# A Fourier-mixing and gated-FFN kernel: the first chunk's work reordered, the chunk-end sums spread wider, and the PSUM seeds put ahead of a sigmoid

## The chip, the cores and the metric

The kernel runs on one core of one Trainium2 chip, in float32 throughout. The metric is the device time of one execution in microseconds (us). The kernel before took 1995.84 us, the median of three runs (1994.73 to 1996.15). Its profiled execution spans 1993.0 us from the first to the last instruction.

## The reference

The input `x` has 8 batches of 3008 rows and 256 features. It goes through a two-dimensional Fourier transform, of which the real part is kept, and then through a gated feed-forward block with 1536 hidden features:

```python
X = np.fft.fft(np.fft.fft(x, axis=1), axis=2).real      # 8 x 3008 x 256
gate = 1.0 / (1.0 + np.exp(-(X @ w_gate)))
val = X @ w_val
out = (gate * val) @ w_out
```

The weights may come as float64, which the kernel converts itself.

## The kernel before, in words

**Fourier part.** The transform over features is linear, so it is multiplied into `w_gate` and `w_val` once (function `merge`), which gives the matrices G1 and G2. Of the transform over the rows only half of the output rows are needed as two parts: `pk` (even) and `qk` (odd). A row k of the output uses P + Q and the mirrored row S-k uses P - Q, with P = pk G1 and Q = qk G2. Each batch therefore gives two tensors with 1505 columns, `pk` and `qk`.

**Chunks, groups, steps.** The 1505 columns are cut into 6 chunks of up to 252. One step of the main loop treats one block of 128 hidden features of one chunk, so a chunk has 12 steps, a batch 72 and the kernel 576. Three steps form a group, whose hidden values h go into one part of the output product.

**One step i** is spread over the engines and over neighbouring steps (the loop at L747). TensorE (PE) computes P for both gates (`front_a`, 8 matmul records pf<-pk), multiplies an older group into the output (`back` of step i-5, 10 records po<-h or po<-sf) and adds Q onto the same PSUM bank (`front_b`, 8 records pf<-qk). Between them P has to be copied away, because S-k needs P - Q: `part` writes it as `ae`. In batch 0, chunk 0 (i < 12) `ae` is made by VectorE (L518); afterwards by ScalarE (L515), and there the bank is also pre-loaded ("seeded") by ScalarE with an edge term (`seed`, L501). Then `gate_a` takes the sigmoid of row k on ScalarE (L534) and forms P - Q for the row S-k as `z` on VectorE (L536 in chunk 0, L539 later). `gate_b` multiplies (L551), takes the S-k sigmoid on ScalarE (L552) and multiplies again (L553). GpSimd (POOL) adds blocks of h into `sf` (L558).

**Output product.** Instead of a plain product a fast scheme with 15 products of 128 x 128 blocks per group is used. It needs sums of weight blocks (`forms`, 11 sums on GpSimd at L311 and 4 scaled copies on ScalarE at L313 for each of four groups), sums of h blocks (`H_SUMS`, L558) and, at the end of a chunk, 20 sums of output blocks (`C_SUMS`, L604), four 32 x 32 transposes (`flip`, L612) and stores (L621, L625). The output banks are copied out of PSUM into the tile `c` by ScalarE as they finish (L582).

**Chunk 0 is special.** In its 12 steps the weights still arrive. There are 18 weight pieces, called jobs here by their index j: two thirds of them go through `merge` (PE, matmuls ps<-...), one third are pieces of `w_out` for `forms`. Each is converted from float64 bits: two activations on ScalarE (`weight_parts`, L260 and L261), three operations on VectorE (`weight_join`, L270, L271, L273) and one add on GpSimd (L275). In the loop job j is converted in step j-9, merged in a later step, and the load of job j+3 is issued when the add of job j has freed its place.

**What sets the order.** All engine queues are in program order, written out by hand: the order of calls in the loop at L747 is the order of the queues. Between engines only semaphores order the work. The lists `use`, `pre`, `side` and `later` are dictionaries or lists of closures which the loop empties at given places in a step; `later` holds the chunk-end sums, of which three are issued per step. Buffers: 3 PSUM banks for pf and ps, 5 for po, one `c` tile (`cp`), one `os` tile (`op`).

Of the kernel before, what the change touches and what calls it, by code (L numbers as in the profile page):

```python
# [7 lines left out]
F32 = mybir.dt.float32  # L8
I32 = mybir.dt.int32
U32 = mybir.dt.uint32  # L10
AF = mybir.ActivationFunctionType
ALU = mybir.AluOpType
# [49 lines left out]
PRODUCTS = ((0, 12), (1, 11), (4, 9), (6, 4), (2, 13), (5, 5), (13, 0), (8, 6), (11, 2), (12, 8), (9, 3),  # L62
            (10, 10), (14, 1), (15, 7), (16, 14))
PLACE = (0, 1, 2, 5, 3, 4, 6, 7, 8, 9, 10, 11, 14, 13, 12)
C_SUMS = (((8, 1, 8, 0), (1, 1, 0, 0), (3, 3, 1, 0), (0, 0, 10, 1), (4, 4, 0, 1), (1, 6, 2, 0),
           (4, 4, 1, 0), (10, 14, 8, 1), (7, 7, 10, 0), (11, 0, 11, 0), (11, 11, 5, 0), (5, 5, 7, 1)),
          ((9, 9, 8, 0), (9, 13, 9, 1), (9, 9, 2, 0), (12, 9, 12, 0), (12, 11, 12, 1), (14, 9, 14, 0),
           (6, 11, 6, 0), (13, 13, 6, 1)))
OUT = (3, 12)

C_LAST = (((8, 1, 8, 0), 0), ((1, 1, 0, 0), 0), ((3, 3, 1, 0), 0), ((1, 6, 2, 0), 1), ((0, 0, 10, 1), 0),
          ((11, 0, 11, 0), 1), ((4, 4, 0, 1), 0), ((4, 4, 1, 0), 0), ((11, 11, 5, 0), 1),
          ((9, 9, 8, 0), 1), ((10, 14, 8, 1), 0), ((7, 7, 10, 0), 0), ((6, 11, 6, 0), 1),
          ((5, 5, 7, 1), 0), ((9, 13, 9, 1), 0), ((9, 9, 2, 0), 0), ((14, 9, 14, 0), 0),
          ((13, 13, 6, 1), 0), ((12, 9, 12, 0), 0), ((12, 11, 12, 1), 0))
HUGE = float((2 ** 24 - 1 - 2 ** 20) * 2.0 ** -7)


@with_exitstack
def kernel(  # L80
# [41 lines left out]
    zp = ctx.enter_context(tc.tile_pool(name="zp", bufs=2))  # L122
    hp = ctx.enter_context(tc.tile_pool(name="hp", bufs=3))
    sp = ctx.enter_context(tc.tile_pool(name="sp", bufs=2))
    cp = ctx.enter_context(tc.tile_pool(name="cp", bufs=1))
    op = ctx.enter_context(tc.tile_pool(name="op", bufs=1))
    psx = ctx.enter_context(tc.tile_pool(name="psx", bufs=8 - NB, space=PSUM))
    pso = ctx.enter_context(tc.tile_pool(name="pso", bufs=1, space=PSUM))
# [52 lines left out]
    ge = const.tile([P, 2, NFT], F32, name="ge")  # L181

    x8 = const.tile([NP, B - 1, 4, NQ], F32, name="x8")
    zero = const.tile([2, 1, NO], F32, name="zero")
    table = const.tile([2, 1], F32, name="table")
    tr = dram.tile([P, 2, NQ, NE + NO], F32, name="tr")
    ed = dram.tile([B, NK + 1], F32, name="ed")
# [23 lines left out]
    def weight_load(j):  # L211


        w, c = jobs[j]
        src = (moe_w_gate, moe_w_val, moe_w_out)[w]
        src = src[2 * c * P : 2 * (c + 1) * P, :] if w == 2 else src[:, c * WC : (c + 1) * WC]
        src = src.rearrange("(c p) f -> p c f", p=P)

        def some(n, pool, tag):

            if tag not in shared:
                shared[tag] = pool.tile([P, n * WC], F32, name=f"w{tag}", tag=tag)
            return shared[tag]

        def home(j):

            if j in (0, 1, 2, 3, 5):
                pool, tag = (hp, "h") if j < 3 else (sp, "sf")
                t = pool.tile([P, 6 * WC], F32, name="raw", tag=tag)
                return t[:, 0 : 4 * WC], t[:, 4 * WC :]  # L230
            if j in (4, 6, 9):
                t = wf[:, {4: 1, 6: 2, 9: 3}[j]].rearrange("p m n -> p (m n)")
                return t[:, 0 : 4 * WC], t[:, 4 * WC : 6 * WC]
            t = some(10, cp, "c")
            if j == 7:
                raw = pqp.tile([P, 4 * WC], F32, name="raw", tag="pk")
                return raw, t[:, 6 * WC : 8 * WC]
            return t[:, 0 : 4 * WC], t[:, 4 * WC : 6 * WC]

        if j < KEEP:  # L240
            raw, ws = home(j)
        else:
            both = some(24, xp, "x4").rearrange("p (i n) -> p i n", n=2 * WC)
            r, i = (j - KEEP) % 3 * 2, 6 + (j - KEEP) % 6
            raw, ws = both[:, r : r + 2].rearrange("p a n -> p (a n)"), both[:, i]
        raw = raw.bitcast(I32).rearrange("p (c f w) -> p c f w", c=2, w=2)
        ws = ws.rearrange("p (c f) -> p c f", c=2)
        WS[j] = ws
        if src.dtype == F32:
            nc.sync.dma_start(out=ws, in_=src)  # L250
        else:
            RAW[j] = raw
            nc.sync.dma_start(out=raw.rearrange("p c f w -> p c (f w)"), in_=src.bitcast(I32))
# [20 lines left out]
                                       op0=ALU.bitwise_and, op1=ALU.bitwise_or)  # L274
        nc.gpsimd.tensor_tensor(wi, wi, lo, op=ALU.add)  # L275

    WO = {}

    def weight_use(j, other=None):
        w, c = jobs[j]  # L280
        if w == 2:
            WO[c] = WS.pop(j)
            for g in range(NG):
                if (3 * g + 2) // 2 == c:
                    forms(g)
        else:
            merge(WS.pop(j), w, c, other)

# [13 lines left out]
    def forms(g):  # L302

        w = [WO[f // 2].rearrange("p f (a h j) -> p f h a j", h=2, j=TB)[:, f % 2]
             for f in range(3 * g, 3 * g + 3)]
        f = wf[:, g].rearrange("p m (a j) -> p m a j", j=TB)

        def block(i):
            return w[i // 2][:, i % 2] if i < 6 else f[:, i - 6]
        for i, (a, b, op) in enumerate(W_SUMS):  # L310
            nc.gpsimd.tensor_tensor(f[:, i], block(a), block(b), op=(ALU.subtract, ALU.add)[op])  # L311
        for i, (a, sign) in enumerate(W_COPIES):
            nc.scalar.mul(f[:, len(W_SUMS) + i], block(a), float(sign))  # L313


    W = {}
# [229 lines left out]
    def gate_b(i):  # L546

        n = cut(i)[2]
        p, fh = i // 3, i % 3
        z, h = Z.pop(i), H[p]  # L550
        nc.vector.tensor_tensor(h[:, fh, 0:n], h[:, fh, 0:n], PF.pop(i)[:, 1], op=ALU.mult)  # L551
        nc.scalar.activation(z[:, 0], z[:, 0], AF.Sigmoid)  # L552
        nc.vector.tensor_tensor(h[:, fh, n:], z[:, 0], z[:, 1], op=ALU.mult)  # L553
        if fh == 1:
            SF[p] = sp.tile([P, 6 * WC], F32, name="sf", tag="sf")[:, 0 : 8 * 2 * CH // 3].rearrange(
                "p (s n) -> p s n", s=8)
        for dst, a, b, op in H_SUMS.get(fh, ()):
            nc.gpsimd.tensor_tensor(block(p, dst), block(p, a), block(p, b),  # L558
                                    op=(ALU.subtract, ALU.add)[op])
# [5 lines left out]
    def back(p, part):  # L565
# [7 lines left out]
        for at_, (hb, wb) in list(enumerate(PRODUCTS))[part * 5 : part * 5 + 5]:  # L573
            t, j = divmod(PLACE[at_], 3)
            mm(PO[t][:, j * R : (j + 1) * R], wf[:, g, wb], block(p, hb), g == 0 and at_ % 3 == 0,
               g == NG - 1)
            if g == NG - 1 and at_ % 3 == 2:
                if t == 0:
                    C[0] = cp.tile([P, 10 * WC], F32, name="c", tag="c")
                    nc.gpsimd.memset(C[0][:, 15 * R : 15 * R + 40], 0.0)  # L580
                if not (last and t == NB - 1):
                    nc.scalar.copy(C[0][:, 3 * t * R : 3 * (t + 1) * R], PO[t][:, 0 : 3 * R])  # L582
        if part == 2:
            del H[p], SF[p]
            if g == NG - 1:
# [2 lines left out]
    def finish(b, c, last):  # L588
# [37 lines left out]
                                      in_=os_[0][a * TB : a * TB + m - full * TB, s, full].rearrange(  # L626
                                          "p h j -> p (h j)"))

        if last:
            for x, e in C_LAST:  # L630
                sum_(*x, engine=(nc.vector, nc.gpsimd)[e])
                if x[0] == 5:
                    flip(0, 0)
                    flip(1, 0)
            for half in range(2):
                flip(half, 1)
                store(half)
            return
        for h in range(2):
            later.extend([lambda x=x: sum_(*x) for x in C_SUMS[h]])  # L640
            later.append(lambda h=h: flip(0, h))
            later.append(lambda h=h: (flip(1, h), h and (store(0), store(1))))

    nc.gpsimd.memset(zero, 0.0)
    nc.scalar.activation(table, zero[:, 0, 0:1], AF.Sigmoid)
    nc.scalar.dma_start(out=dt, in_=dtab.rearrange("(c p) d -> p c d", p=P))  # L650
    for j in range(2):
        weight_load(j)
# [42 lines left out]
    def at(i, *fs):  # L695
        side.setdefault(i, []).extend(fs)
# [2 lines left out]

    pre, use = {}, {}  # L700
    for j in range(9, len(jobs)):
        pre.setdefault(j - 9, []).append(lambda j=j: weight_parts(j))
        at(j - 9, lambda j=j: weight_join(j))
        if KEEP <= j < len(jobs) - 3:
            at(j - 9, lambda j=j: weight_load(j + 3))
    for j in range(3, len(jobs)):
        w, c = jobs[j]
        use.setdefault(2 * c + (-3, -2, 1)[w], []).append(lambda j=j: weight_use(j))


    i0 = NFT
# [34 lines left out]

    for i in range(count):  # L747
        front_a(i)
        if i:
            gate_a(i - 1)  # L750
        part(i)
        if i:
            gate_b(i - 1)
        for f in use.pop(i, []):
            f()
        if i >= 5:
            back((i - 5) // 3, (i - 5) % 3)
        front_b(i)
        for f in pre.pop(i, []):
            f()  # L760
        for j in range(max(i0, i + 1), min(count, i + 3)):
            if j not in PF:
                seed(j)
        for f in later[0:3]:
            f()
        del later[0:3]
        for f in side.pop(i, []):
            f()
    gate_a(count - 1)
    gate_b(count - 1)  # L770
    for i in range(count, count + 5):
        back((i - 5) // 3, (i - 5) % 3)
    for f in later:
        f()


# [47 lines left out]
```

## Time and profile before

| | before |
|---|---|
| time, median of 3 | 1995.84 us |
| span of the profiled execution | 1993.0 us |
| TensorE busy | 1945.6 us (98%) |
| VectorE busy | 1538.4 us (77%) |
| ScalarE busy | 1395.6 us (70%) |
| GpSimd busy | 1627.1 us (82%) |
| mean granted TensorE clock | 0.993 |

A busy share is the share of the span in which an engine had an instruction in flight. The slices of the profile cut the span into 40 equal parts and give the same share for each. A table by windows gives busy time for stretches chosen by the reader, with the granted clock of TensorE. A timeline lists instructions in order of time; in square brackets stands how long the engine was idle before, and what ended that. Matmul records of one kind that follow each other are merged into one row with their number.

### The profile page before, as it was taken

The page shows a single profiled execution, that of the slowest core. Times are in us where ns is not written, and L with a number is a line of the kernel's source. Part 1 is how long each engine was busy: PE and PEld are TensorE (multiplying, and loading weights), DVE is VectorE, ACT ScalarE, POOL GpSimd, SP SyncE. Part 2 cuts the span into 40 slices and gives each one's busy share as a digit, 9 for nine tenths or more (in the row PEclk, how much of TensorE's full clock was granted, in tenths as well). Part 3 has the DMA queues.
Part 4 walks back from the last instruction along what each step waited for, and adds up shares of the span by engine and source line. Part 5 has one row for each costly group of instructions (what it writes and reads, how often), then busy time and mean ns, then how long its engine had stood idle before and what let it go on. Part 6 is the DMA issues. An engine that isn't in the chain of part 4 may idle for free.

```text
span 1993.0 us, 34353 instructions
## 1 busy us (share of the span) xinstructions
PE 1945.6 (98%) x11232; PEld 1793.0 (90%) x11232; DVE 1538.4 (77%) x3061; ACT 1395.6 (70%) x3198; POOL 1627.1 (82%) x2878
## 2 busy tenths in 40 slices
PE   6799999999999999999999999999999999999997
PEld 4689889998999899998999989999899999999997
DVE  7668778886788778787878877788678876877776
ACT  3467767776777667776777767777677776777775
POOL 3788988897888878897889878888788886777776
PEclk8999999999999999999999999999999999999999
DMA  7253413112012020211112021111210110011011
GB/s 266 86 132 90 139 29 109 45 25 80 14 46 56 16 77 14 60 44 49 43 25 79 15 77 24 45 49 20 79 19 14 20 21 14 14 23 18 14 21 24
DMA packets 171414, 101.40 MB, mean 51 GB/s; under 512 B 133860, under 2 KB 163172, under 8 KB 168556
## 3 DMA queue, kind: packets, MB, share of 16 engines
q1 hardware_dynamic: 169294, 98.64, 19.7%
q8 instruction: 88, 1.44, 0.3%
q10 hardware_dynamic: 1940, 0.56, 0.1%
q14 instruction: 92, 0.75, 0.1%
HBM read 74.39 MB, written 50.18 MB: 63 GB/s over the span
## 4 chain that ended last, share of the span: by engine, by line
PE 79%; DVE 12%; ACT 5%; POOL 2%; issue 1%; DMA 1%; SPq 0%; POOLq 0%; DVEq 0%; ACTq 0%
PE pf L131 40%; PE po L131 33%; DVE c L604 6%; PE ev L131 4%; DVE z L539 3%; DVE h L553 2%; ACT z L552 2%; ACT pf L501 1%; PE od L131 1%; ACT ae L515 1%; DMA x<-in_xf_dram 1%; POOL wf L311 1%; ACT c L582 1%; POOL sf L558 1%; PE ps L131 1%
## 5 line engine op out<-in xcount | busy, mean ns | idle before, releaser
L558 POOL TENSOR_TENSOR sf<-h 128x168 f32<-128x168 f32 (+1 forms) x960 | 540.4, 581 | 239.3 <-DVE h L553 239.3
L558 POOL TENSOR_TENSOR sf<-h,sf 128x168 f32<-128x168 f32 (+1 forms) x1152 | 644.9, 579 | 56.1 <-DVE h L553 56.1
L131 PE MATMUL pf<-qk,G 128*128 128x252 f32 (+1 forms) x2304 | 587.8, 378 | 7.7 <-DVE ae L518 4.3
L131 PE MATMUL pf<-pk,G 128*128 128x252 f32 (+1 forms) x2304 | 582.7, 376 | 0.0
L501 ACT ACTIVATE pf<-ek,ge 128x252 f32<-128x252 f32 (+1 forms) x1128 | 535.8, 475 | 18.4
L539 DVE TENSOR_TENSOR z<-ae,pf 128x504 f32<-128x504 f32 (+1 forms) x564 | 376.5, 668 | 221.2 <-ACT h L534 220.5
L604 DVE TENSOR_TENSOR c<-c 128x168 f32<-128x168 f32 (+1 forms) x950 | 520.9, 564 | 16.9 <-ACT c L582 3.6
L131 PE MATMUL po<-sf,wf 128*128 128x168 f32 (+1 forms) x3072 | 530.9, 306 | 0.0
L131 PEld LDWEIGHTS pf<-pk,G 128*128 128x128 f32 x2304 | 437.1, 190 | 51.8 <-issue 2.3
L131 PE MATMUL po<-h,wf 128*128 128x168 f32 (+1 forms) x2688 | 477.2, 306 | 6.2 <-POOL wf L311 4.6
L131 PEld LDWEIGHTS po<-sf,wf 128*128 128x128 f32 x3072 | 473.9, 190 | 8.4
L131 PEld LDWEIGHTS po<-h,wf 128*128 128x128 f32 x2688 | 428.2, 190 | 23.6 <-POOL wf L311 5.1
L131 PEld LDWEIGHTS pf<-qk,G 128*128 128x128 f32 x2304 | 408.3, 190 | 44.8 <-ACT ae L515 12.5
L515 ACT ACTIVATE ae<-pf 128x504 f32<-128x504 f32 (+1 forms) x564 | 331.0, 587 | 147.6 <-PE pf L131 142.1
L553 DVE TENSOR_TENSOR h<-z 128x252 f32<-128x252 f32 (+1 forms) x576 | 335.7, 583 | 115.7 <-ACT z L552 114.5
L552 ACT ACTIVATE z<-z 128x252 f32<-128x252 f32 (+1 forms) x576 | 236.2, 410 | 217.8 <-DVE z L539 194.0
L534 ACT ACTIVATE h<-pf 128x252 f32<-128x252 f32 (+1 forms) x576 | 213.2, 370 | 81.7 <-PE pf L131 68.7
L551 DVE TENSOR_TENSOR h<-h,pf 128x252 f32<-128x252 f32 (+1 forms) x576 | 233.1, 405 | 0.0
L582 ACT COPY c<-po 128x504 f32<-128x504 f32 (+1 forms) x239 | 127.5, 574 | 2.9 <-PE po L131 2.9
L558 POOL TENSOR_TENSOR sf<-sf 128x168 f32<-128x168 f32 (+1 forms) x192 | 109.7, 571 | 15.0
L558 POOL TENSOR_TENSOR sf<-sf,h 128x168 f32<-128x168 f32 (+1 forms) x192 | 112.8, 588 | 0.0
L131 PE MATMUL ev<-st,x 63*128 63x376 f32 (+4 forms) x372 | 98.1, 416 | 7.6 <-DVE x L335 7.6
(103 smaller groups left out, 793.6 us busy)
## 6 DMA issues: line engine op xcount, KB each, us to landing
x<-xr SPq DMA_DIRECT2D x14, 1536.0 KB
out_dram<-os SPq DMA_DIRECT2D x380, 56.0 KB
xr<-in_xf_dram SPq DMA_DIRECT2D x14, 768.0 KB
xr<-in_xf_dram SPq DMA_DIRECT2D x35, 256.0 KB
ek<-ed SPq DMA_DIRECT2D x39, 126.0 KB
out_dram<-os SPq DMA_DIRECT2D x288, 7.0 KB
x<-in_xf_dram SPq DMA_DIRECT2D x2, 1512.0 KB
tr<-in_stab_dram SPq DMA_DIRECT2D x2, 1129.5 KB
```

The source lines that it names most:

```text
L131: nc.tensor.matmul(o, l, r, start=start, stop=stop, skip_group_check=True)
L311: nc.gpsimd.tensor_tensor(f[:, i], block(a), block(b), op=(ALU.subtract, ALU.add)[op])
L501: nc.scalar.activation(PF[i][:, g], EK[i // NFT], AF.Copy, scale=ge[:, g, f : f + 1])
L515: nc.scalar.activation(AP[i], PF[i], AF.Copy, scale=2.0)
L534: nc.scalar.activation(H[p][:, fh, 0:n], PF[i][:, 0], AF.Sigmoid)
L539: nc.vector.tensor_tensor(z[:, :, ::-1], AP.pop(i), PF[i], op=ALU.subtract)
L551: nc.vector.tensor_tensor(h[:, fh, 0:n], h[:, fh, 0:n], PF.pop(i)[:, 1], op=ALU.mult)
L552: nc.scalar.activation(z[:, 0], z[:, 0], AF.Sigmoid)
L553: nc.vector.tensor_tensor(h[:, fh, n:], z[:, 0], z[:, 1], op=ALU.mult)
L558: nc.gpsimd.tensor_tensor(block(p, dst), block(p, a), block(p, b), op=(ALU.subtract, ALU.add)[op])
L582: nc.scalar.copy(C[0][:, 3 * t * R : 3 * (t + 1) * R], PO[t][:, 0 : 3 * R])
L604: engine.tensor_tensor(t[:, dst * R : (dst + 1) * R], *v, op=(ALU.subtract, ALU.add)[op])
```

## The change

The change has these parts.

1. Chunk 0, `ae` ahead of `z`: in steps i < 12 `part(i)` is issued before `gate_a(i - 1)`, so VectorE makes the copy of P of step i before the P - Q of step i-1.
2. Chunk 0, conversions in the middle of a step: `weight_parts` and `weight_join` are called together ahead of the step's merges, instead of activations after `front_b` and the joins at the end of the step.
3. The forms of the weights start sooner (steps 1, 4, 9, 10 instead of 3, 5, 9, 11), are issued in two pieces of 6 and 5 sums in consecutive steps, and those of groups 2 and 3 go from GpSimd to VectorE.
4. Chunk ends: the two different lists of sums become one, in the order in which the last chunk had them; per step 2 or 3 closures are issued in turn instead of 3, and `c` has two buffers. The stores of the two halves follow their own transposes. The copies of banks 1 and 3 go from ScalarE to VectorE. What is left in `later` at the end of the loop is issued ahead of the last `back` calls instead of behind them.
5. Seeds: one seed per step, for step i+1, issued between `ae` of step i and the S-k sigmoid of step i-1; before, seeds were issued at the end of a step, up to two steps ahead.
6. To make room for the second `c`, the tile `zero` goes to DRAM (written once from a small tile by a GpSimd DMA), `sf` shrinks from 1536 to 1344 columns, and two weight pieces (jobs 3 and 5) take another home.

```diff
@@ tiles
-    cp = ctx.enter_context(tc.tile_pool(name="cp", bufs=1))
+    cp = ctx.enter_context(tc.tile_pool(name="cp", bufs=2))
...
-    zero = const.tile([2, 1, NO], F32, name="zero")
+    nil = op.tile([2, 1, NO], F32, name="nil", tag="os")
+    zero = dram.tile([2, 1, NO], F32, name="zero")
@@ forms
-        for i, (a, b, op) in enumerate(W_SUMS):
-            nc.gpsimd.tensor_tensor(f[:, i], block(a), block(b), op=(ALU.subtract, ALU.add)[op])
-        for i, (a, sign) in enumerate(W_COPIES):
-            nc.scalar.mul(f[:, len(W_SUMS) + i], block(a), float(sign))
+        engine = nc.gpsimd if g < 2 else nc.vector
...
+        def some(lo, hi):
+            for i, (a, sign) in enumerate(W_COPIES if lo == 0 else ()):
+                nc.scalar.mul(f[:, len(W_SUMS) + i], block(a), float(sign))
+            for i, (a, b, op) in list(enumerate(W_SUMS))[lo:hi]:
+                engine.tensor_tensor(f[:, i], block(a), block(b), op=(ALU.subtract, ALU.add)[op])
+        return [lambda lo=lo: some(lo, lo + 6) for lo in range(0, len(W_SUMS), 6)]
@@ back
-                    nc.scalar.copy(C[0][:, 3 * t * R : 3 * (t + 1) * R], PO[t][:, 0 : 3 * R])
+                    (nc.vector.tensor_copy if t % 2 else nc.scalar.copy)(
+                        C[0][:, 3 * t * R : 3 * (t + 1) * R], PO[t][:, 0 : 3 * R])
@@ finish
-        for h in range(2):
-            later.extend([lambda x=x: sum_(*x) for x in C_SUMS[h]])
-            later.append(lambda h=h: flip(0, h))
-            later.append(lambda h=h: (flip(1, h), h and (store(0), store(1))))
+        for x, e in C_SUMS:
+            add(lambda x=x, e=e: sum_(*x, engine=(nc.vector, nc.gpsimd)[last and e]))
+            if x[0] == 5:
+                add(lambda: flip(0, 0))
+                add(lambda: flip(1, 0))
+        for half in range(2):
+            add(lambda half=half: (flip(half, 1), store(half)))
@@ schedule of the weights
-        pre.setdefault(j - 9, []).append(lambda j=j: weight_parts(j))
-        at(j - 9, lambda j=j: weight_join(j))
+        pre.setdefault(j - 9, []).append(lambda j=j: weight_round(j))
...
-        use.setdefault(2 * c + (-3, -2, 1)[w], []).append(lambda j=j: weight_use(j))
+        i = (0, 1, 4, 7, 9, 10)[c] if w == 2 else 2 * c - 3 + w
+        use.setdefault(i, []).append(lambda j=j: weight_use(j))
@@ main loop
     for i in range(count):
         front_a(i)
+        if i < NFT:
+            part(i)
         if i:
             gate_a(i - 1)
-        part(i)
+        if i >= NFT:
+            part(i)
+        if i0 <= i + 1 < count:
+            seed(i + 1)
         if i:
             gate_b(i - 1)
-        for f in use.pop(i, []):
+        todo = pre.pop(i, []) + use.pop(i, [])
+        for f in [parts_.pop(0)] + todo if parts_ else todo + [lambda: parts_ and parts_.pop(0)()]:
             f()
         if i >= 5:
             back((i - 5) // 3, (i - 5) % 3)
         front_b(i)
-        for f in pre.pop(i, []):
+        for f in later[0 : 2 + i % 2]:
             f()
-        for j in range(max(i0, i + 1), min(count, i + 3)):
-            if j not in PF:
-                seed(j)
-        for f in later[0:3]:
-            f()
-        del later[0:3]
+        del later[0 : 2 + i % 2]
         for f in side.pop(i, []):
             f()
     gate_a(count - 1)
     gate_b(count - 1)
+    for f in later:
+        f()
     for i in range(count, count + 5):
         back((i - 5) // 3, (i - 5) % 3)
-    for f in later:
-        f()
```

## The prediction

> **What bounds the kernel now.** I read the slices first, then the table by windows of the first 130 us, the timeline of each engine there, the list of waits, and last the timelines of one chunk end and of the kernel's end.
>
> ```profile
> PE   6799999999999999999999999999999999999997
> POOL 3788988897888878897889878888788886777776
> ```
>
> The table by windows (from:to, length, busy time and count of PE, PEld, DVE, ACT, POOL, then granted clock, DMA share, GB/s):
>
> ```profile
> 60.00:70.00 10.00, 7.59 (x34) 6.10 (x34) 9.54 (x18) 6.19 (x19) 9.50 (x15) 1.00 0.39 106
> 80.00:90.00 10.00, 3.77 (x21) 2.96 (x19) 7.06 (x14) 2.88 (x7) 9.92 (x19) 0.93 0.29 83
> 90.00:100.00 10.00, 10.00 (x39) 8.89 (x40) 3.66 (x8) 3.06 (x8) 6.91 (x11) 0.73 0.18 53
> 110.00:120.00 10.00, 7.11 (x33) 6.58 (x33) 3.13 (x8) 4.42 (x13) 9.92 (x23) 0.83 0.46 156
> 120.00:130.00 10.00, 10.00 (x60) 9.44 (x59) 5.54 (x10) 7.98 (x19) 9.92 (x21) 1.00 0.45 143
> ```
>
> TensorE is the bound from 120 us on: 9 in every slice, 60 matmuls per 10 us. Only chunk 0, the chunk ends and both ends of the kernel leave it anything. In chunk 0 it does 21 to 39 matmuls per 10 us, and in three windows its clock is cut (0.93, 0.73, 0.83). GpSimd is full there (9.92). The timeline of TensorE names the large waits:
>
> ```profile
> 75.77 1.12 PE L131 MATMUL po<-h,wf 128*128 128x168 f32 x6 [1.69 <-POOL wf L311]
> ...
> 89.95 3.78 PE L131 MATMUL ps<-wx,dt 128*128 128x256 f32 x8 [5.51 <-POOL wx L275]
> ...
> 112.97 2.04 PE L131 MATMUL po<-h,wf 128*128 128x168 f32 x6 [2.89 <-POOL wf L311]
> ```
>
> All three end on GpSimd: twice on forms, once on the conversion add of job 14. Each of the last two is followed by half clock (the eight ps records take 3.78 us instead of 1.89). The pf<-pk of step 0 starts at 49.28, that of step 12 at 116.20 (same timeline): 66.9 us. At full pace it would be 12 x 1.70 (pf) + 9 x 1.73 (merges) + 7 x 1.425 (back) = 46 us, so chunk 0 loses 21 us. The GpSimd chain into the largest wait:
>
> ```profile
> 58.98 1.29 POOL L275 TENSOR_TENSOR wx<-wx 128x512 int32<-128x512 int32 x1 [2.65 <-DMA ge<-G]
> ...
> 88.63 1.27 POOL L275 TENSOR_TENSOR wx<-wx 128x512 int32<-128x512 int32 x1
> ```
>
> These are the adds of jobs 10 and 14. Between them GpSimd was idle only 0.42 us. Next a line of the list of waits (total us, times, longest), and one chunk end in the timeline of all engines:
>
> ```profile
> PEld pf L131 <- ACT ae L515: 12.5, 36, 1.2
> ```
>
> ```profile
> 661.69 1.06 PE L131 MATMUL pf<-qk,G 128*128 128x252 f32 x4
> 662.18 0.66 DVE L539 TENSOR_TENSOR z<-ae,pf 128x504 f32<-128x504 f32 x1
> 662.88 0.41 ACT L552 ACTIVATE z<-z 128x252 f32<-128x252 f32 x1 [1.30 <-DVE z L539]
> 663.27 0.98 ACT L501 ACTIVATE pf<-ek,ge 128x252 f32<-128x252 f32 x2
> 663.86 1.84 DVE L604 TENSOR_TENSOR c<-c 128x168 f32<-128x168 f32 x3
> 664.45 0.58 ACT L515 ACTIVATE ae<-pf 128x504 f32<-128x504 f32 x1
> 665.08 1.12 PE L131 MATMUL pf<-qk,G 128*128 128x252 f32 x4
> ```
>
> The three sums take 1.84 us, so VectorE needs 3.45 us from one z to the next (662.18 to 665.63). ScalarE waits 1.30 us for z, does the seeds behind it, is late with ae, and TensorE starts its next qk 3.39 us after the last instead of 3.12. At the end of the kernel:
>
> ```profile
> 1974.48 0.32 SPq L621 DMA_DIRECT2D out_dram<-os  x1
> ...
> 1981.63 0.43 SPq L625 DMA_DIRECT2D out_dram<-os  x1
> ...
> 1983.78 0.94 DVE L612 STREAM_TRANSPOSE os<-c 128x256 f32<-128x256 f32 x2
> ```
>
> The 16 stores of the chunk before last take 7.6 us to issue; the last chunk's first transposes write the same single `os` tile.
>
> [...] L604 takes 0.31 us alone (at 668.19) and 0.61 beside GpSimd. [...] half clock follows the waits of 5.51 and 2.89 us, not that of 1.69.
>
> **Chunk 0: forms and conversions.** Job 14's merge stays in step 7 and its add is still queued behind the same GpSimd work: adds 10 to 13, two sets of h sums and one more half group, forms 0, forms 1. The spreading only permutes this list. So the chain stays near 30 us (58.98 to 89.90, less 0.42 idle) and only its start moves. Job 9's activations now go ahead of the step-0 G copies, so its join no longer holds up VectorE in step 1 (it waited 2.11 us at 53.30). I get job 10's join about 0.9 us sooner. Job 14's merge starts at about 58.1 + 30.4 = 88.5 instead of 89.95: 1.5 us. Bounds: 0 (start unmoved) and 4[...]. Both forms waits vanish as waits (1.69 and 2.89), but the first one is inside the 88.5: TensorE would just arrive at step 7 sooner, near 81, and wait there. The loads of jobs 13 to 17 wait on SP for adds 10 to 14, with the `ge` reads queued behind them; they are late too, but only for work ahead of that same wait.
>
> **Chunk 0: ae ahead of z.** It removes the waits of 0.4 to 1.3 us on L518. In steps 1 to 4 VectorE itself is full (9.54 of 10 us): ae 0.78 + z 0.59 + two products 0.66 + join 1.54[...]. So little comes of it before step 7, and what does is inside the wait for job 14.
>
> **Chunk 0: after step 7.** From the merge on, TensorE needs 3.4 (merge, half clock) + 1.5 + 0.85, so pf<-pk of step 8 starts near 94.2 (before 96.73). Step 8 needs 4.86, step 9 3.1. Steps 10 and 11 carry forms 2 on VectorE, which this trace does not show for 128 columns. [...] I take 0.3 each when overlapped: 6 add 1.5 to 1.8 us to about 2.0 of ae, z and products and 0.4 of waiting, so a step is 3.6 to 4.2. The instruction held up is the next ae, and behind it front_b. Step 12 then starts near 109.8, instead of 116.20. The 2.89 us wait and its half clock (1.7 us) are in this. **Chunk 0 in sum: 6 us gained, between 1 and 11.**
>
> **Chunk ends.** Of the 36 waits on ae (12.5 us), one stretch at 214 us (1.1 us) belongs to the edge sums and stays. The others cost 0.27 to 0.33 each (3.39 or 3.45 against 3.12): 35 x 0.30 = 10.5 us. The seeds leave the chain z, S-k sigmoid, seeds, ae: 0.92 us more room, three times the lateness. 2.5 sums instead of 3 take 0.3 us per step from VectorE; two copies (0.6 to 0.67 each, as z L539 with the same size) come back once per chunk, while ScalarE has one copy per step instead of two. I take 9 us, bounds 5 and 10.5. The cost: the S-k sigmoid, its product and GpSimd's sums come 0.9 us later per step. GpSimd's sums are needed three steps on, so this is hidden. The second `c` buffer hides the longer list (24 closures / 2.5 = 9.6 steps).
>
> **The end.** Eight steps after the second-last chunk 20 of 24 closures are issued; two sums and both transposes with all stores now stand behind the last L553 (1975.84). So the first store goes from 1974.48 to about 1977.9, the last lands 3.4 us later (its packets ended near 1982.8, so 1986.3), and the last chunk's transposes wait for them: 1986.4 instead of 1983.78. **Loss 2.6 us**, between 0.5 and 3. The tile `zero` in DRAM, the moved homes and `sf`: nothing, since its small DMA runs while VectorE still waits for weights, and no added operation lies in the loop.
>
> **Sum:** 1995.84 - 6 - 9 + 2.6 = 1983.4 us.
>
> **Rivals.** A: the GpSimd chain doesn't move and forms on VectorE cost what they save, so chunk 0 gains nothing: 1995.84 - 9 + 2.6 = 1989.4. For it: GpSimd at 9.92. Against it: the third wait ends on work that leaves GpSimd. Chance 0.20. B: the three waits (1.69 + 5.51 + 2.89) and the half clock (0.07 + 0.27 + 0.17, at 10 us each: 5.1) all vanish: 1995.84 - 15.2 - 9 + 2.6 = 1974.2. Against it: the chain count. Chance 0.14. C, slower: the seed, now only one step ahead, becomes what pf<-pk waits for. From 120.37 (ae) I count its end at 121.84, TensorE reaches the next pk at 122.45: 0.6 us of room. If ScalarE's issue and semaphores ate that and 0.05 us more, 564 steps would lose 28 us: 1983.4 + 28 = 2011. Against it: ScalarE idles about 1 us per step. Chance 0.08.
>
> **Numbers.** The likeliest case has 0.58 and spreads over 1978 to 1988. The range 1973 to 1991 holds it, most of A and of B. Faster by over 0.2% (under 1991.85): 0.58 + 0.15 of A + 0.14 = 0.87; within: 0.05 of A and 0.02 of C = 0.07; slower 0.06.
>
> **What would show it.** Right: the merge of job 14 starts at 87 to 89.5 after a wait of 5 us or more with half clock; pf<-pk of step 12 near 110; weight loads of pf waiting for ScalarE's ae fall from 36 to under 8; the last transposes wait for a DMA. Wrong: a wait of pf<-pk on seeds in most steps (C), no long wait in step 7 (B), or new waits of po on GpSimd's sums.

## The result and the profile after

The changed kernel takes 1984.95 us, the median of four runs (1984.49 to 1987.29), against 1995.99 us before. The ratio is 0.9947, with a 95% interval of 0.993 to 0.9964: faster, by 7 to 14 us. The prediction was 1983.4 us. A second measurement, beside other kernels, gave 1985.4 against 1994.89 us (0.9955, 0.9938 to 0.9971).

The slices of the profile after show nearly the same picture as before, as they must for half a per cent. Only the second digit of TensorE, which holds most of chunk 0, has changed.

```profile
PE   6899999999999999999999999999999999999997
POOL 3879898997889878997889868998688886777775
```

For a change of this size the profile has to be cut at landmarks that both kernels have. I took four: the first `pf<-pk` of step 0, that of step 12, the start of the last group of TensorE records (14 times `po<-sf`), and the last chunk's first pair of transposes.

| stretch (us) | before | after | after again | predicted |
|---|---|---|---|---|
| start to step 0 | 49.28 | 52.20 | 50.72 | no change |
| step 0 to step 12 (chunk 0) | 66.92 | 62.66 | 61.90 | -6 |
| step 12 to the last TensorE group | 1862.9 | 1851.8 | 1851.6 | -9 |
| last TensorE group to the transposes | 4.68 | 7.28 | 7.41 | +2.6 |
| transposes to the end | 9.22 | 9.30 | 9.26 | no change |

**Chunk 0.** The table by windows, with the columns of the one before:

```profile
80.00:90.00 10.00, 5.22 (x26) 4.01 (x25) 8.22 (x15) 2.79 (x7) 9.92 (x18) 0.98 0.45 120
90.00:100.00 10.00, 8.14 (x31) 7.14 (x32) 3.56 (x6) 2.25 (x5) 9.14 (x13) 0.68 0.20 53
110.00:120.00 10.00, 9.55 (x53) 8.65 (x54) 9.51 (x24) 5.56 (x17) 4.13 (x9) 1.00 0.47 156
```

GpSimd (POOL) is still full up to the large wait. From 110 us on it has 4.13 us of work instead of 9.92, and VectorE has 9.51 instead of 3.13: the forms have changed sides. TensorE does 53 matmuls there instead of 33. The waits in TensorE's timeline:

```profile
91.86 3.78 PE L127 MATMUL ps<-wx,dt 128*128 128x256 f32 x8 [6.08 <-POOL wx L274]
...
109.95 1.12 PE L127 MATMUL pf<-qk,G 128*128 128x252 f32 x4 [1.38 <-DVE ae L521]
...
112.94 1.12 PE L127 MATMUL po<-h,wf 128*128 128x168 f32 x6 [0.45 <-DVE wf L315]
```

The wait ahead of job 14's merge is there, with half clock behind it (granted clock 0.50 from 91.86 to 95.40 us; before, 0.50 from 89.95 to 93.53); those of 1.69 and 2.89 us on forms are gone, and a smaller pair on VectorE has come. GpSimd's chain into the large wait:

```profile
61.05 1.30 POOL L274 TENSOR_TENSOR wx<-wx 128x512 int32<-128x512 int32 x1 [4.00 <-ACT wf L313]
...
90.53 1.28 POOL L274 TENSOR_TENSOR wx<-wx 128x512 int32<-128x512 int32 x1
```

From the add of job 10 to the end of the add of job 14 this is 30.76 us, against 30.92 before. It begins 8.85 us behind step 0 instead of 9.70.

**Chunk ends.** The line of the list of waits that counted 36 waits (12.5 us) now reads:

```profile
PEld pf L127 <- ACT ae L518: 2.3, 2, 1.9
```

Only the stretch at the edge sums is left. One chunk end in the timeline of all engines:

```profile
649.13 0.67 DVE L542 TENSOR_TENSOR z<-ae,pf 128x504 f32<-128x504 f32 x1
...
650.77 1.84 DVE L607 TENSOR_TENSOR c<-c 128x168 f32<-128x168 f32 x3
652.54 0.67 DVE L542 TENSOR_TENSOR z<-ae,pf 128x504 f32<-128x504 f32 x1
...
654.22 0.56 DVE L607 TENSOR_TENSOR c<-c 128x168 f32<-128x168 f32 x2
654.71 0.67 DVE L542 TENSOR_TENSOR z<-ae,pf 128x504 f32<-128x504 f32 x1
```

With three sums between them VectorE takes 3.41 us from one z to the next (649.13 to 652.54), with two it takes 2.17. TensorE's two steps take 6.25 (pf<-qk at 649.43 and 655.68).

**The end.** The timeline of all engines there (SPq: an issue on a DMA queue of SP):

```profile
1967.94 0.67 DVE L584 COPY c<-po 128x492 f32<-128x492 f32 x1 [1.00 <-PE po L127]
...
1968.52 2.48 DVE L607 TENSOR_TENSOR c<-c 128x164 f32<-128x164 f32 x6
...
1972.38 0.42 SPq L628 DMA_DIRECT2D out_dram<-os  x1
1973.90 0.77 DVE L615 STREAM_TRANSPOSE os<-c 128x256 f32<-128x256 f32 x2 [1.72 <-DMA out_dram<-os]
```

The first sums start 1.90 us behind the start of the last TensorE group (1966.62), before 1.08 us (1980.18 against 1979.10); then the transposes wait 1.72 us for the stores. The chain that ended last is now 94% TensorE, before 79%.

### The profile page after: what moved, and what is told of

Its sections match the earlier page's. It is cut to its first block, busy times and chain, and to the rows that moved or that the text cites. A ratio compares the mean times of both kernels' runs of the same rounds, so it can differ in the third digit from the quotient of the medians.

```text
span 1983.2 us, 34391 instructions
## 1 busy us (share of the span) xinstructions
PE 1936.4 (98%) x11232; PEld 1790.2 (90%) x11232; DVE 1488.3 (75%) x3179; ACT 1338.3 (67%) x3102; POOL 1624.8 (82%) x2857
## 4 chain that ended last, share of the span: by engine, by line
PE 94%; DMA 2%; DVE 2%; POOL 1%; ACT 1%; issue 0%; SPq 0%; ACTq 0%; DVEq 0%; POOLq 0%
PE pf L127 48%; PE po L127 41%; PE ev L127 4%; DMA ge<-G 1%; DMA st<-in_stab_dram 1%; PE od L127 1%; PE ps L127 0%; DVE wf L315 0%; DMA wx<-in_moe_w_val_dram 0%; DVE ae L521 0%; POOL sf L560 0%; POOL wf L315 0%; DVE z L539 0%; DMA raw<-in_moe_w_gate_dram 0%; DMA wx<-in_moe_w_gate_dram 0%
## 5 line engine op out<-in xcount | busy, mean ns | idle before, releaser
L560 POOL TENSOR_TENSOR sf<-h 128x168 f32<-128x168 f32 (+1 forms) x960 | 550.8, 592 | 233.1 <-DVE h L556 233.0
L556 DVE TENSOR_TENSOR h<-z 128x252 f32<-128x252 f32 (+1 forms) x576 | 293.7, 510 | 377.0 <-ACT z L555 376.4
L607 DVE TENSOR_TENSOR c<-c 128x168 f32<-128x168 f32 (+1 forms) x950 | 467.1, 514 | 8.5
L537 ACT ACTIVATE h<-pf 128x252 f32<-128x252 f32 (+1 forms) x576 | 218.7, 380 | 172.3 <-PE pf L127 160.2
L555 ACT ACTIVATE z<-z 128x252 f32<-128x252 f32 (+1 forms) x576 | 230.8, 401 | 76.7 <-DVE z L542 46.5
L560 POOL TENSOR_TENSOR sf<-sf 128x168 f32<-128x168 f32 (+1 forms) x192 | 114.3, 595 | 15.1
L560 POOL TENSOR_TENSOR sf<-sf,h 128x168 f32<-128x168 f32 (+1 forms) x192 | 107.5, 560 | 0.0
L127 PEld LDWEIGHTS ev<-st,x 63*128 63x128 f32 (+1 forms) x372 | 66.8, 188 | 37.0 <-issue 7.3
```

The source lines that it names most:

```text
L127: nc.tensor.matmul(o, l, r, start=start, stop=stop, skip_group_check=True)
L537: nc.scalar.activation(H[p][:, fh, 0:n], PF[i][:, 0], AF.Sigmoid)
L607: engine.tensor_tensor(t[:, dst * R : (dst + 1) * R], *v, op=(ALU.subtract, ALU.add)[op])
```

## The experiments

Each kernel was timed in five rounds beside the kernel before; "before" in this section is the median of the same set (1994.42, 1994.89 and 1996.73 us for the three sets). Every kernel computes the whole output.

### Part 6 alone, and the start

```diff
 (kernel before)
-    zero = const.tile([2, 1, NO], F32, name="zero")
+    nil = op.tile([2, 1, NO], F32, name="nil", tag="os")
+    zero = dram.tile([2, 1, NO], F32, name="zero")
...
+    nc.gpsimd.dma_start(out=zero, in_=nil)
     (and the homes of jobs 3 and 5, and the size of sf, as in the change)
```

> The kernel before with part 6 alone (the tile of zeros in DRAM, the new homes of jobs 3 and 5, the smaller sf). In the changed kernel the first pf<-pk started at 52.20 us instead of 49.28, after a wait of 2.79 us for the sine table and half clock behind it. Theory A, the spread of the landing of the first loads: the time stays within 0.1% of the kernel before (about 1996), and the first pf<-pk starts near 49 to 50 us in most profiles of this set, whichever of the kernels it is. Rival, part 6 delays the sine table (one more DMA, other order of use): about 2.9 us slower, near 1998.9, and every profile of a kernel with part 6 shows the first pf<-pk near 52, every one without it near 49.

Measured: 1995.2 against 1994.42 us, ratio 1.0003 (0.9995 to 1.0012); step 0 at 49.59 us. The delay of 2.9 us in the profile after is therefore not shown to come from part 6. The rival's sharp form falls too: with part 6 step 0 starts anywhere from 49.59 to 52.63 us in the profiles of this study, without it at 49.28 and 50.92. My own "49 to 50 in most" was too narrow. The four profiles in which it starts after 52 us have a wait of the first Fourier matmuls for the sine table of 1.7 to 2.8 us; but one with a wait of 1.85 us starts at 50.08, so that is not all of it. On the other hand, ten of the twelve profiles with part 6 show such a wait and neither of the two without it. A shift by part 6 of up to 2.4 us, the upper end of the interval, stays open.

### The two halves of the change

First the changed kernel with parts 1 to 3 undone, then the kernel before with parts 1 to 3 alone:

```diff
 (parts 4 to 6 alone: changed kernel)
-        if i < NFT:
-            part(i)
         if i:
             gate_a(i - 1)
-        if i >= NFT:
-            part(i)
+        part(i)
...
 (and forms(g) whole on GpSimd, weight_parts behind front_b, weight_join
  at the end of the step, the old steps of use; the other kernel is the reverse)
```

> The changed kernel with its chunk 0 undone (parts 1 to 3 as in the kernel before), so parts 4, 5 and 6 alone. Theory: the changes are separate in time and add up. The trace of the changed kernel has 11.1 us less between step 12 and the last matmul and 2.6 us more behind it, so about 8.5 us faster than before: 1987.5 (with the late start of 2.9 us, if that comes from part 6: 1990.4). Rival, that chunk 0 brings most of it: 1993 or more.

> The kernel before with parts 1 to 3 alone (ae ahead of z in chunk 0, conversions in the middle of a step, forms sooner, in two pieces, groups 2 and 3 on VectorE). Theory: 4.3 us faster than before, 1991.7, all of it from the first pf<-pk to that of step 12 (66.9 to 62.6 us), with the merge of job 14 still waiting 5 to 6 us for GpSimd. Rival A of the prediction (forms on VectorE cost what they save): within 1 us of before. If it's the full 6 us of the prediction, parts 4 to 6 took 1.7 us away in chunk 0.

Measured: parts 4 to 6 alone 1987.29 us, 7.1 less than before (ratio 0.9973, 0.9961 to 0.9986); parts 1 to 3 alone 1991.67 us, 2.75 less (0.9988, 0.998 to 0.9997). Together 9.9 us, and the two measurements of the whole change gave 11.0 and 9.5: they add up as far as the intervals tell, which are wide (2.8 to 7.8 us and 0.6 to 4.0 us for the halves). In the traces the stretch from step 12 to the last group is 1851.5 us with parts 4 to 6 and 1864.2 with parts 1 to 3, and the end 7.29 and 4.68.

Chunk 0 brings less than the pair of profiles said (4.3). The reason is in the two other profiles with the old chunk 0. Part 6 alone, TensorE's timeline:

```profile
112.15 1.12 PE L131 MATMUL po<-h,wf 128*128 128x168 f32 x6 [2.89 <-POOL wf L314]
```

This is the same wait of 2.89 us as in the kernel before, but the six records behind it take 1.12 us and not 2.04: no half clock (granted 1.00 from 110 to 120 us; in the kernel before, 0.50 from 112.97 to 114.81). So do those of parts 4 to 6 alone, behind 2.88 us (1.00 from 110 to 120 us). The half clock behind the large wait is shorter there too: from the merge to step 8 it is 5.6 and 5.8 us, in the kernel before 6.8 (granted clock from 90 to 100 us: 0.83, 0.83 and 0.73). Chunk 0 takes 64.4 and 64.5 us there, not 66.9. The mean of the three kernels with the old chunk 0 is 65.3 us; that of the eight with the changed one (forms on VectorE and GpSimd's order both as in the change) is 62.5. The difference, 2.8 us, agrees with the 2.75 timed.

### Forms of groups 2 and 3 on GpSimd again

```diff
-        engine = nc.gpsimd if g < 2 else nc.vector
+        engine = nc.gpsimd
```

> The changed kernel with the forms of groups 2 and 3 on GpSimd again (still in two pieces and at the new steps). In the changed kernel six forms sums on VectorE take 2.6 us beside GpSimd's work and hold up ae of steps 10 and 11 (waits of 1.38 and 0.45 us). Theory: on GpSimd a piece takes 3.3 us or more behind the h sums, so the waits of po on forms come back in step 11 and perhaps 14 (1 to 3 us), while the 1.38 on ae goes: 0 to 2 us slower than the changed kernel. Rival A of the prediction (forms on VectorE cost what they save or more): 0.5 to 2 us faster.

Measured: 1990.3 against 1996.73 us before (0.9964, 0.9952 to 0.9977), and 5.2 us above a kernel of the same set that has the changed chunk 0 (one `c` buffer, below). Chunk 0 takes 66.0 us. The wait on forms is back and is longer than it ever was:

```profile
114.52 2.05 PE L127 MATMUL po<-h,wf 128*128 128x168 f32 x6 [3.57 <-POOL wf L315]
```

That is more than the 0 to 2 us that I expected. Against the mean of 65.3 us for the old chunk 0, the other edits of chunk 0 bring nothing that shows without this one. So the gain there needs the move to VectorE, and rival A of the prediction has fallen. Whether the move would pay alone was not run.

### GpSimd's order in chunk 0

```diff
-        todo = pre.pop(i, []) + use.pop(i, [])
-        for f in [parts_.pop(0)] + todo if parts_ else todo + [lambda: parts_ and parts_.pop(0)()]:
+        todo = pre.pop(i, []) + ([lambda: h_sums(i - 1)] if 0 < i <= NFT else []) + use.pop(i, [])
+        for f in todo + [lambda: parts_ and parts_.pop(0)()]:
     (h_sums: the sums at L560, taken out of gate_b for i < NFT)
```

> The changed kernel with another order of GpSimd's work in chunk 0: the sums of h (sf) are issued behind the conversion add of the step, and a piece of the forms at the end of the step's list instead of its start. The prediction said that the merge of job 14 waits for a queue of GpSimd work that the change only permutes. Theory: with the add of job 14 ahead of two sets of h sums and of forms 1 it ends 5 to 7 us sooner (from 30.8 us behind the add of job 10 to 24 to 26), the wait of 6 us before that merge falls under 2 us without half clock, and since the displaced sums are needed later, 3 to 6 us of it stay: 1979 to 1982. Rival, the merge then waits for something else (the load of the weights, VectorE's join, or the h sums wanted by po): within 1.5 us of the changed kernel, with a wait of as many us a step later.

Measured: 1982.33 us (0.9933, 0.9919 to 0.9947), beside the changed kernel's 1985.4: 3.1 us less. The two intervals overlap, so it is the trace that carries the argument. The waits in TensorE's timeline:

```profile
84.08 1.99 PE L127 MATMUL ps<-wx,dt 128*128 128x256 f32 x8 [2.78 <-POOL wx L274]
...
91.27 1.97 PE L127 MATMUL ps<-wx,dt 128*128 128x256 f32 x8 [2.07 <-ACT G L296]
```

The add of job 14 now ends at 84.02 us, 24.9 us behind the start of the add of job 10 (59.10), and the wait ahead of its merge is 2.78 us with full clock (1.00 from 80 to 90 us; the eight ps records take 1.99 us). So the large wait was indeed the queue on GpSimd, and an order that puts the add first shortens it where the change's order did not; the wait is longer than the "under 2 us" expected. Part of the gain goes to a wait a step later (2.07 us) and to 2.17 us on `ae` in step 10. Chunk 0 takes 59.7 us, 2.8 less than the mean of 62.5.

### Which part freed the chunk ends

Four kernels make a square: 2 and 3 closures in turn or 3 in every step, seeds at the new or the old place.

```diff
 (three per step)
-        for f in later[0 : 2 + i % 2]:
+        for f in later[0:3]:
...
 (old seeds: the call ahead of gate_b goes, and behind front_b comes)
+        for j in range(max(i0, i + 1), min(count, i + 3)):
+            if j not in PF:
+                seed(j)
```

> The changed kernel once more, beside the other runs of this set, so that differences of 1 to 3 us from it can be read on one chip. Expected: 1984 to 1985, 10 to 11 us faster than before. Theory on the start: a first pf<-pk anywhere between 49 and 52 us, by the landing of the sine table.

> The changed kernel with the seeds back where they were (at the end of the step, up to two steps ahead); the sums stay spread at 2 or 3 a step. It tells the two parts of the chunk-end gain (11 to 12 us from step 12 to the last matmul) apart. Theory: the seeds are the larger part, since they take 0.92 us out of the chain z, S-k sigmoid, ae, while 2 or 3 sums instead of 3 take 0.3 us from VectorE in every other step only, so that the steps with 3 sums are late as before: half or more of the gain is lost, 5 us or more slower than the changed kernel, with 15 or more waits of pf on ae. Rival, the spreading alone does it: within 1.5 us of the changed kernel, under 8 waits on ae.

> The changed kernel with 3 closures per step throughout instead of 2 and 3 in turn (seeds as changed). Theory: the room that the seeds leave (0.92 us) is three times the lateness (0.3 us), so 3 sums per step cost nothing, and the list of the second-last chunk is empty in time: as the run with 3 per step in the last 8 steps only, 1 to 2 us faster than the changed kernel. Rival, the spreading is needed: 36 or so waits of pf on ae again, 5 to 10 us slower than the changed kernel.

> The fourth cell of a square: three closures per step and the seeds at their old place (spread with new seeds 1985.4, spread with old seeds 1983.4, three with new seeds 2001.0). Theory now: VectorE needs 3.45 us for a step with three sums against TensorE's 3.12, and that repeats in every such step, so no slack in ScalarE's chain can hide it; 2 and 3 in turn is what removes it, whatever the place of the seeds. Then this run has waits of pf on ae as before (30 or more), and takes 1993 to 2001. Rival: the new place of the seeds is what makes three per step bad (sigmoid and product come later): this run within 2 us of the changed kernel.

| closures per step | seeds | time (us) | ratio to before (95%) | step 12 to last group | waits of pf on ScalarE's ae |
|---|---|---|---|---|---|
| 2 and 3 | new | 1985.40 | 0.9955 (0.9938 to 0.9971) | 1851.6 | 2 |
| 2 and 3 | old | 1983.41 | 0.9938 (0.9925 to 0.9951) | 1852.0 | 4 |
| 3 | new | 2000.98 | 1.0030 (1.0021 to 1.0039) | 1869.6 | 45 |
| 3 | old | 2003.26 | 1.0034 (1.0022 to 1.0046) | 1875.2 | 60 |

My theory fell twice, in the second and in the third row. With the rest as changed, 2 and 3 instead of 3 is worth 15 to 20 us. With 2 and 3 in turn the place of the seeds makes no difference that these runs can tell. With three per step the times do not tell the two places apart either, but the profile with the new place has fewer waits (the first of these two lines from the lists of waits), and its stretch from step 12 to the last group is 5.6 us shorter:

```profile
PEld pf L127 <- ACT ae L518: 14.4, 45, 0.8
PEld pf L127 <- ACT ae L518: 23.1, 60, 1.2
```

The fourth row lies 2 us over what was expected of it. The timeline of VectorE in the last row's kernel shows why:

```profile
622.38 0.67 DVE L542 TENSOR_TENSOR z<-ae,pf 128x504 f32<-128x504 f32 x1
...
624.05 1.84 DVE L607 TENSOR_TENSOR c<-c 128x168 f32<-128x168 f32 x3
625.82 0.67 DVE L542 TENSOR_TENSOR z<-ae,pf 128x504 f32<-128x504 f32 x1
...
627.50 1.88 DVE L607 TENSOR_TENSOR c<-c 128x168 f32<-128x168 f32 x3
629.30 0.67 DVE L542 TENSOR_TENSOR z<-ae,pf 128x504 f32<-128x504 f32 x1
```

z follows z after 3.44 and 3.48 us, step upon step. TensorE needs 3.12. A shorter chain on ScalarE can give a lead once, and VectorE eats 0.3 us of it in each step with three sums; a lead therefore helps only where the row of such steps is short enough. That fits the few us that the new place saves in the third row, and is argued from these rows. Two sums and three in turn bring it to 6.15 us for two steps of 6.25 (652.54 to 658.69 in the changed kernel).

With three per step both kernels are also 6 to 7 us slower than the kernel before, which has three per step too. What they have beyond it is the two copies on VectorE and the other order of the list. In the trace a copy of 0.67 us (616.14) stands right ahead of the first three sums, and z follows z there after 4.28 us (614.13 to 618.41). That this is the cause is argued from those rows and not shown; no kernel with three per step and the copies on ScalarE was run, nor the kernel before with nothing but 2 and 3 in turn.

### One buffer for c

```diff
-    cp = ctx.enter_context(tc.tile_pool(name="cp", bufs=2))
+    cp = ctx.enter_context(tc.tile_pool(name="cp", bufs=1))
```

> The changed kernel with one buffer for c. In its trace the closures of a chunk end run from 648.0 to 676.1 us and the first copy of the next chunk into c comes at 681.2 us, 5 us later. Theory: the second buffer hides nothing, since the longer list is done before c is written again: the time stays within 1 us of the changed kernel, and part 6 isn't needed for part 4. Rival, as the prediction had it (the second buffer hides the longer list): copies wait for transposes at each chunk end, and some us are lost, 0.2 or more per chunk, 10 us in all.

Measured: 1985.08 us (0.9944, 0.9931 to 0.9956), as the changed kernel. VectorE's timeline of this kernel:

```profile
674.88 0.77 DVE L615 STREAM_TRANSPOSE os<-c 128x256 f32<-128x256 f32 x2
681.22 0.67 DVE L584 COPY c<-po 128x504 f32<-128x504 f32 x1
```

The list is done at 675.65 us, 5.6 us before VectorE's first copy of the next chunk. ScalarE writes into `c` earlier, which I had not counted: in the changed kernel its first copy comes at 678.03 us, which still leaves 1.9 us behind the end of the list there (676.13). The second buffer, and part 6 which makes room for it, bring no time.

### The end of the kernel

```diff
-        for f in later[0 : 2 + i % 2]:
+        n = 3 if i >= count - 8 else 2 + i % 2
+        for f in later[0:n]:
             f()
-        del later[0 : 2 + i % 2]
+        del later[0:n]
```

> The changed kernel with three closures per step in the last 8 steps only, so that the list of the second-last chunk is empty before the last matmul. Theory: the last transposes wait for the stores of the second-last chunk only because 4 of the 24 closures are still in the list; with 24 of 24 issued the wait is gone and the time from the last matmul to the last transposes is about 2.9 us again instead of 5.5: 2.6 us faster than the changed kernel, 1982.4. Rival: the 16 issues on SP (7.6 us) end too late all the same, since the transposes of the second half still come in the last steps: less than 1 us gained, or the third sum per step costs it again at this chunk end.

Measured: 1983.77 us, ratio 0.9952 (0.9939 to 0.9964), which the times alone do not tell from the changed kernel (0.9947 and 0.9955). The trace shows the term, at 1.5 us and not 2.6: the wait of the transposes on the stores is gone, and they start 5.81 us behind the start of the last group instead of 7.28. The last group itself takes 2.69 us instead of 2.11, as the third sum delays the h that GpSimd and then TensorE need.

### A version that beats both

```diff
 (GpSimd's order and three closures in the last 8 steps as above, and)
-                    (nc.vector.tensor_copy if t % 2 else nc.scalar.copy)(
+                    (nc.vector.tensor_copy if t % 2 and not last else nc.scalar.copy)(
```

> The changed kernel with three edits together: GpSimd's order in chunk 0 (h sums behind the conversion add, 3 us gained alone), three closures per step in the last 8 steps (the stores of the second-last chunk issued in time, 1.5 us in the trace), and the last chunk's copies all on ScalarE as before (first sums 0.8 us sooner). Theory: these lie apart in time and add up, 3 + 1.5 + 0.8 = 5.3 us under the changed kernel, 1979 to 1980, with the last transposes 4.7 us behind the start of the last group of matmul records as in the kernel before (5.8 with the second edit alone, 7.3 in the changed kernel). Rival: something else ends the kernel (GpSimd's five sums there), and only the 3 us of chunk 0 stay.

Measured: 1980.88 us, ratio 0.9922 (0.991 to 0.9934): 15.9 us less than before, and 4.2 less than the one-buffer kernel of the same set, which times like the change (5.3 expected); the slowest of its runs, 1983.08, is faster than the fastest of that kernel, 1984.16. Step 0 to step 12 takes 59.8 us, as with GpSimd's order alone. The transposes start 5.18 us behind the start of the last group; the 0.5 us over the kernel before is that group's own 0.58 us.

## Why the prediction was right, and where it was not

**In sum.** 1984.95 us against 1983.4, inside the range, in the likeliest case: the chain on GpSimd kept the large wait, and the late steps at the chunk ends went. That the sum came so close is in part luck. Chunk 0 gave about 3 us less than predicted and the chunk ends 2 us more, and the reason that I put first for the chunk ends is not the one that holds. Rivals A (1989.4), B (1974.2) and C (2011) did not come about.

**Chunk 0: 6 us predicted, 2.8 measured.** The steps up to the merge held. The chain "stays near 30 us": 30.76. Its start: 0.9 us sooner predicted, 0.85 measured. The merge starts 1.0 us sooner behind step 0 (40.67 before, 39.66 after) against 1.5, inside the bounds of 0 and 4, of which the 4 was an estimate with no trace behind it. That little would come of `ae` ahead of z before step 7, and that the wait would swallow it, held too. VectorE took 3.81 to 5.02 us from one z to the next there before (54.83 to 72.68), where 1.70 + 1.73 = 3.43 us was counted for TensorE; step 6 starts 2.35 us sooner behind step 0 (28.30 and 25.95), and the merge behind it 1.0.

The terms after the merge were mis-sized. I counted 21.3 us from the merge to step 12 and it was 23.0. Of these 1.7 us, 1.1 lie in steps 10 and 11, which carry the forms on VectorE (8.7 us together, about 7.6 in my count). Six forms, "1.5 to 1.8 us", took 2.6 (106.45 to 109.04), and the next ae, with front_b behind it, waited. The 0.3 us that I took for each was an estimate that no trace of the kernel before shows. In the changed kernel one takes up to 0.65 us beside GpSimd and 0.28 alone (112.80). The other 0.6 is half clock that reached into the po records behind the merge (2.04 us at 95.44, granted clock 0.76); in the second profile of the same kernel it did not (1.59). And I counted the half clock behind the wait of 2.89 us as a cost of the kernel before. It is one in that profile (2.04 us for the six records), and not in the two others that have the wait (1.12).

**Chunk ends: 9 us predicted, 11.1 measured in the pair of profiles.** The term was the right one: of 564 steps, 32 are 0.25 to 0.4 us shorter than before, 10.2 us in all, where I had counted 35 times 0.30 and taken 9 of it. The reason that I put first is the step that failed: "The seeds leave the chain ... three times the lateness". It set a lead of 0.92 us against the lateness of a single step, while VectorE falls 0.3 us behind in every step with three sums (3.44 against 3.12 us), and several of them follow each other. In the kernel before, these 32 steps lie in 15 of the 47 chunk ends; the others, with as many sums, have none of them. I read that as a lead that lasts there; no run tests it. The 2.5 sums per step, which I had put down as a help, keep VectorE's rate within TensorE's (6.15 against 6.25 us for two steps), and with them the place of the seeds makes no difference that shows. "The second `c` buffer hides the longer list" failed as well: one buffer does.

**The end: 2.6 us predicted, 2.6 measured.** The mechanism is right, the transposes wait for the stores. The terms are not quite: the stores ended sooner than I put them (last issue at 1972.38), so the wait is 1.72 us, and 0.8 us come from the first sums starting later behind the last TensorE group, with the last copy now at the end of VectorE's queue. I had costed the delay by that copy at nothing.

**The start** was not in the sum; its spread of 3 us is as large as what the two profiles differ by there.

**Two readings of lines** in the prediction are not right, though no term of the sum rests on them alone. TensorE does up to 55 matmuls per 10 us in chunk 0 (from 100 to 110 us), not 39 at most. The sum at 668.19 was not alone: a GpSimd sum of h was in flight at its start (667.27 to 668.31). One that is alone, at 1974.92 in the changed kernel, takes 0.33 us, so the comparison with 0.61 stands.

## What to carry to other kernels

Compare the rates first: where an engine needs 3.45 us per step beside one that needs 3.12, set a lead that a shorter chain gives against the lateness of all such steps in a row, not of one. Taking work out of those steps does away with the lateness itself. Where a wait ends on a full queue, ask which of the entries ahead of the awaited one is needed later than it, since changing that order adds no work; part of the wait can come back where the displaced entries are needed. Before a difference of a few us is explained from two profiles, look at the same stretch in every profile that shares it.

## What the runs showed of the hardware

**Half clock behind a wait did not go by its length alone.** Behind 2.89 us the six po records took 2.04 us in the kernel before (granted clock 0.50) and 1.12 with part 6 alone (1.00). Behind 2.78 us the eight ps records took 1.99 us (reordered GpSimd), behind 2.80 in the last version 3.68. Behind 2.18 us in the last version four pf<-qk records took 1.65 us and the four pf<-pk records after them 1.88; behind 2.17 with reordered GpSimd these took 1.12 and 1.01. In chunk 0, waits of 3.57 us and over were followed by half clock, at least in part, each time (3.44 to 3.78 us for the eight ps records, against the 1.99 above; 2.05 us for six po records behind 3.57). So half clock came right behind a wait of 2.18 us and full clock behind one of 2.89; what decides between them the runs do not show.

**The first loads land with a spread.** The wait for the sine table is 0.5 to 2.8 us where it shows at all (ten of fourteen profiles). Step 0 moves by up to 3 us between profiles, and by 1.5 us between the two of the changed kernel (52.20 and 50.72). In the two profiles that waited 2.66 and 2.79 us half clock followed (3.42 and 3.51 us for six records instead of 2.14; in the second, the changed kernel, granted clock 0.59 from 41.11 to 44.41).
